# RWKV-7 scan and a quick-GELU MLP on one core: padded rows for the channel sums of the decays, and another order for the first third of a hand-listed program

## The chip, the cores and the metric

The kernel runs on one core of one Trainium2 chip. The metric is the time of one execution on the device in microseconds; lower is better. TensorE (PE in the profile) multiplies and writes to PSUM; VectorE (DVE), ScalarE (ACT) and GpSimd (POOL) do the elementwise work; SyncE (SP) issues nearly all DMA transfers from one queue.

## The reference

For each of 4 batches and 8 heads a 40x40 state runs over 768 steps; its readings, put side by side, go through an MLP with the activation h * sigmoid(1.702 h).

```python
B, H, S, D = 4, 8, 768, 40
for t in range(S):
    y[:, :, t] = einsum('bhd,bhde->bhe', r_t, state)
    Sa = einsum('bhde,bhe->bhd', state, a_t)
    state = state * w_t[:, :, None, :] - einsum('bhd,bhe->bhde', Sa, b_t) + einsum('bhd,bhe->bhde', v_t, k_t)
x = y.transpose(0, 2, 1, 3).reshape(3072, 320)
h = x @ w_in                                  # 320 x 2048
out = (h / (1 + exp(-1.702 * h))) @ w_out     # 2048 x 320
```

All is float32 but the two weights, which arrive in float64.

## The kernel before

**Units.** The steps are cut into 12 chunks of 64, the batches into 2 pairs; a chunk of a pair is a unit, 24 in all, unit i being chunk i // 2 and pair i % 2. For each unit the kernel loads the decays w, and a, k, b, r, v, and takes the logarithm of w (line 536). `by_time` and `by_channel` (lines 552 and 560) add up the logarithms along the chunk by matmuls with the triangular mask `edges`, once with time on the partitions (psum tile ps_cum) and once with channels (ps_cumc). Exponentials of the sums give FT, GT, wch and G, with which a, b, k are scaled (lines 629 to 637). `by_channel` is used for the units below BY_PE = 4; the others load w a second time in channel order (wc) and use a scan on VectorE. Then come the scores A, RV and N (ps_A, ps_RV, ps_N), five levels of a blockwise inverse (ps_level), its off-diagonal parts (ps_Q, ps_T), the solve (ps_B, ps_X) and the reading (ps_y), whose result x goes to DRAM and comes back transposed as xT_all. In units 0 to 3 a level is a matmul group from PT and EX into ps_level, a transpose of ps_level on DVE into EX (line 733) and a copy to PT on ACT or DVE (line 794). Unit i needs the state that unit i - 2 left (ps_zT, ps_rz). When both units of a chunk are back, the MLP of the chunk runs: ps_up, the activation, ps_down.

**Weights.** The float64 weights come as eight pieces of 1.3 MB, each by four transfers into a raw buffer, and are made into float32 by one ACT instruction (line 457, "rebased"), three on DVE (461, 465, 469) and one on POOL (473, "joined"). The raw buffers are shared: pieces 0, 5 and 7 use one, 3 and 6 another.

**The order.** Every step is a task with a number, given by the order in which the program adds it. The text ORDER lists all 2,709 tasks in the order in which they are issued; a token is the task's number, the letter of its engine (p TensorE, a ScalarE, d VectorE, g GpSimd, s SyncE) and, for a task that uses PSUM, which of four pairs of banks it gets. Each engine runs its tasks strictly in this order. For SyncE the digit behind the letter is a window: with 4, this transfer waits until all but the last four issued ahead of it have landed; without a digit it waits for none.

The numbers that matter here:

| tasks | what they are |
| --- | --- |
| 0, 1, 2, 91 | load of w for units 0 to 3 |
| 5, 6, 7, 8, 9 and 10 to 14 | loads of ak, b, rv, v (RV), time (k and b by time) for units 0 and 1 |
| 15 to 18, 24 to 27, 33 to 36, 42 to 45 | loads of weight pieces 0 to 3, four quarters each |
| 19, 28, 37, 46, 55, 64, 73, 82 | "rebased" of weight pieces 0 to 7 |
| 23, 32, 41, 50, 59, 68, 77, 86 | "joined" of weight pieces 0 to 7 |
| 87, 88 and 141, 142 | ps_cum and ps_cumc of units 0 and 1 |
| 93, 94, 95, 96, 97 and 148 to 152 | scaling of a, b, k (by channel) and k, b (by time), units 0 and 1 |
| 100 and 101 | ps_RV of unit 0 and its masking on DVE |
| 103 and 158 | ps_N of units 0 and 1 |
| 107, 110, 113, 116, 119 / 162 ... 174 / 290 ... 302 | levels of units 0, 1 and 2 |
| 126, 128, 134, 136 / 181, 183, 189, 191 | ps_Q, ps_T, ps_X, ps_y of units 0 and 1 |
| 138, 139, 140 / 193, 194, 195 | x, x to DRAM, x read back, units 0 and 1 |
| 351, 353, 363 | ps_A, ps_RV and the second level of unit 3 |
| 196 to 205, 207 to 216 | first two quarters of ps_up of the first chunk |

Of the kernel before, what the change touches and what calls it, by code (L numbers as in the profile page):

```python
# [121 lines left out]
200p2 58d 468p1 201p2 368d0 469a 473s 202p2 476s 203p2 67d 387p0 477s 470a1 490d 204p2 68g 480s 339a 205p2 369p1 388d0 206a2  # L122
215p3 371d1 218p0 219p0 56d 472s4 216p3 483g 71s4 220p0 217a3 471d 81s4 221p0 482d 79s 311p2 222p0 370a1 223p0 224p0 312d2 225p0
340d 372p3 229p1 478s4 376a3 230p1 57d 378a3 324p2 560s4 377a3 59g 226p0 78s4 375a3 325d2 231p1 73a 232p1 227p0 373d3 326p2 374d
228a0 389p3 484g 479s3 327d2 338s4 240p0 529d 390a3 481g 328d2 379p3 233p1 380a3 329d 234p1 391p2 485g 241p0 556s4 392d2 80s4
# [118 lines left out]
2690p3 2691p3 2692p3 2693p3 2694p3 2698p1 2695a3 2699p1 2696d3 2700p1 2697s 2701p1 2702p1 2703p1 2704p1 2705p1 2706d1 2707d1  # L244
2708s
"""


@with_exitstack
def rwkv7_gelu_quick(ctx: ExitStack, tc: tile.TileContext, time_d, v_d, w_d, wc_d, ak_d, b_d, rv_d, w_in, w_out, out):  # L250
    nc = tc.nc
    H, D, S = 8, 40, out.shape[0] // 4
    DM = H * D
    C = 64
    MID = C // 2
    NU = time_d.shape[0]
# [8 lines left out]
    BY_PE = 4  # L265
# [110 lines left out]
    for t in logw_t:  # L376
        nc.gpsimd.memset(t[:, DM:], 0.0)
# [772 lines left out]
```

## Time and profile before

| | us |
| --- | --- |
| median of 3 runs | 680.82 (679.36 to 682.35) |
| the profiled execution's own time | 679.49 |
| its span, first to last instruction | 677.7 |
| TensorE matmul busy | 649.6 (96%) |
| VectorE, ScalarE, GpSimd busy | 449.7, 329.1, 175.7 |
| DMA | 69.74 MB, mean 103 GB/s |

Matmul busy time is the union of pipelined instructions, so a full TensorE is not TensorE at its peak. Nearly every matmul of the program is recorded on line 301, a helper, and every DMA on line 331, so groups are told apart by their tiles. The profile counts two instructions for each float32 matmul of the program. "Idle before" in a row is the time for which the engine had nothing to run ahead of this group, and what ended it.

### The profile page before, as it was taken

Reading aid. Unit: us, or ns where it says so; the run is one execution under the profiler, and the core shown is the slowest. Engines: PE = TensorE matmul, PEld = TensorE weight load, DVE = VectorE, ACT = ScalarE, POOL = GpSimd, SP = SyncE. Lnnn points to the kernel's source line nnn. Section 1 sums busy time; section 2 is a strip of 40 time slices with the busy share of each in tenths; the row PEclk is TensorE's granted clock in tenths of the full one; section 3 lists DMA queues with packets and bytes.
Section 4 is the critical chain, followed back from the end, with each engine's and each line's share of the span. In section 5 each row is a group of like instructions: output and inputs, shape, how many; then the busy total and the mean of one; then the engine's idle time right before and its main releaser. Section 6 shows DMA issues by size and latency. Waiting matters only on the chain.

```text
span 677.7 us, 42447 instructions
## 1 busy us (share of the span) xinstructions
PE 649.6 (96%) x19616; PEld 568.7 (84%) x19616; DVE 449.7 (66%) x916; ACT 329.1 (49%) x681; POOL 175.7 (26%) x201
## 2 busy tenths in 40 slices
PE   5777999999999999999999999999999999999997
PEld 4667787787999997888888899999889798799896
DVE  5777779777867668757776687868656766675001
ACT  3676745634564655654545445455344454263010
POOL 6541443324123123123113211322411421300000
PEclk9979999999999999999999999999999999999999
DMA  6875753415324314432404513513412411200200
GB/s 208 295 255 160 226 172 97 129 42 152 107 64 131 94 58 124 114 107 65 124 14 131 149 35 108 155 33 107 140 38 62 130 53 45 69 15 14 60 13 21
DMA packets 35473, 69.74 MB, mean 103 GB/s; under 512 B 5472, under 2 KB 14816, under 8 KB 35296
## 3 DMA queue, kind: packets, MB, share of 16 engines
q1 hardware_dynamic: 35216, 66.99, 32.9%
q8 instruction: 154, 2.52, 1.6%
q14 instruction: 23, 0.19, 0.1%
q10 hardware_dynamic: 80, 0.04, 0.0%
HBM read 59.15 MB, written 7.86 MB: 99 GB/s over the span
## 4 chain that ended last, share of the span: by engine, by line
PE 88%; DMA 6%; DVE 2%; issue 1%; SPq 1%; ACT 1%; DVEq 0%; ACTq 0%
PE ps_up L301 31%; PE ps_down L301 29%; PE ps_level L301 8%; PE ps_y L301 5%; PE ps_B L301 4%; PE ps_X L301 2%; PE ps_N L301 2%; PE ps_rz L301 1%; PE ps_RV L301 1%; PE ps_A L301 1%; PE ps_zT L301 1%; SPq L331 1%; DMA w_sb<-in_w_in 1%; PE ps_cum L301 1%; PE ps_T L301 1%
## 5 line engine op out<-in xcount | busy, mean ns | idle before, releaser
L301 PE MATMUL ps_up<-xT_all,w_sb 64*64 64x256 f32 x3840 | 253.3, 377 | 2.1 <-issue 1.3
L301 PE MATMUL ps_down<-w_sb,g 64*64 64x320 f32 (+1 forms) x3200 | 241.5, 419 | 0.2 <-ACT zr L879 0.2
L301 PEld LDWEIGHTS ps_up<-xT_all,w_sb 64*64 64x64 f32 x3840 | 170.8, 133 | 18.8 <-issue 2.1
L301 PEld LDWEIGHTS ps_down<-w_sb,g 64*64 64x64 f32 x3200 | 142.5, 133 | 31.6 <-issue 0.4
L1000 ACT ACTIVATE g<-ps_up 128x1024 f32<-128x1024 f32 x48 | 49.2, 1025 | 46.3 <-PE ps_up L301 45.8
L719 POOL TENSOR_TENSOR EX<-ES,quads 128x512 f32<-128x512 f32 x30 | 39.7, 1324 | 116.4 <-DVE ES L712 77.7
L761 ACT COPY W<-ps_level 128x512 f32<-128x512 f32 x56 | 32.8, 585 | 67.7 <-PE ps_level L301 66.0
L301 PEld LDWEIGHTS ps_level<-W,EX 64*64 64x64 f32 x2560 | 60.0, 134 | 5.4 <-DVE T L840 0.2
L763 DVE TENSOR_TENSOR E<-two,ps_level 128x256 f32<-128x256 f32 x80 | 33.1, 415 | 36.5 <-ACT W L761 32.3
L301 PE MATMUL ps_level<-W,EX 64*64 64x64 f32 (+1 forms) x2560 | 56.8, 217 | 0.0
L717 ACT ACTIVATE EX<-ES,quads 128x256 f32<-128x256 f32 x82 | 37.2, 501 | 31.9 <-DVE ES L712 31.3
L629 POOL TENSOR_TENSOR ak<-ak,FT 128x512 f32<-128x512 f32 x17 | 23.0, 1353 | 77.2 <-DMA ak<-in_ak 54.4
L301 PEld LDWEIGHTS ps_level<-PT,EX 64*64 64x64 f32 x1280 | 30.7, 138 | 11.5 <-DVE EX L733 3.3
L301 PE MATMUL ps_level<-PT,EX 64*64 64x64 f32 (+2 forms) x1280 | 32.5, 234 | 6.9 <-DVE EX L733 5.0
L712 DVE STREAM_TRANSPOSE ES<-E 128x256 f32<-128x256 f32 x80 | 35.3, 443 | 4.4
L301 PE MATMUL ps_y<-RV,kh 64*64 64x104 f32 (+1 forms) x768 | 35.4, 247 | 0.9 <-DVE M L917 0.9
L301 PE MATMUL ps_y<-M,bh 64*64 64x104 f32 (+1 forms) x768 | 35.5, 247 | 0.7 <-DVE M L917 0.5
L901 ACT COPY B<-ps_B 128x416 f32<-128x416 f32 (+1 forms) x35 | 17.2, 493 | 34.4 <-PE ps_B L301 34.2
L301 PEld LDWEIGHTS ps_y<-RV,kh 64*64 64x64 f32 x768 | 29.6, 133 | 3.2 <-DVE M L917 1.5
L917 DVE TENSOR_TENSOR M<-ps_X,later 128x832 f32<-128x832 f32 (+1 forms) x24 | 23.9, 995 | 10.2 <-PE ps_X L301 10.0
L301 PE MATMUL ps_B<-RV,A 64*64 64x104 f32 (+1 forms) x768 | 29.2, 252 | 0.8 <-issue 0.8
L637 POOL TENSOR_TENSOR kh<-time,G 128x320 f32<-128x320 f32 x18 | 16.2, 901 | 51.2 <-PE ps_y L301 34.6
(133 smaller groups left out, 1099.0 us busy)
## 6 DMA issues: line engine op xcount, KB each, us to landing
ak<-in_ak SPq DMA_DIRECT2D x48, 160.0 KB
rv<-in_rv SPq DMA_DIRECT2D x48, 160.0 KB
time<-in_time SPq DMA_DIRECT2D x24, 320.0 KB
xT_all<-x_dram SPq DMA_DIRECT2D x48, 160.0 KB
wc<-in_wc SPq DMA_DIRECT2D x20, 264.0 KB
logw<-in_w SPq DMA_DIRECT2D x24, 160.0 KB
RV<-in_v SPq DMA_DIRECT2D x24, 160.0 KB
b<-in_b SPq DMA_DIRECT2D x48, 80.0 KB
```

The lines of the kernel that those rows point to most:

```text
L301: nc.tensor.matmul(o, lhsT, rhs, start=start, stop=True, skip_group_check=True)
L331: begun.append(queue.dma_start(dst, src).ins)
L629: plan.add(R, {"DVE": 690.0, "POOL": 1270.0, "sbuf": True}, lambda t: of(t.engine).tensor_mul(ahT(), ahT(), FT_of(i)), reads=T("ak", "FT") ...
L637: plan.add(R + 4, {"POOL": 870.0, "DVE": 490.0, "sbuf": True}, lambda t, n=n, dst=dst: of(t.engine).tensor_mul(dst(i)[:, :, :D], by_head(t ...
L712: plan.add(rank, dve(256), lambda t: nc.vector.transpose(ES(n), source(t)), writes=[key("ES", n, 6)], **reads)
L717: nc.scalar.activation(dst[:, :, h], ES(n), ACT.Copy, scale=quads[:, h, :1])
L719: of(t.engine).tensor_mul(dst, ES(n).unsqueeze(2).to_broadcast([128, 8, 2, 32]), quads.unsqueeze(1).to_broadcast([128, 8, 2, 32]))
L761: plan.add(rank, any2(512), lambda t: copy(t.engine)(tiles_of(W(n + 1)), blocks(psum(t, ""), 64)), writes=[key("W", n + 1, 5)], pair=pair)
L763: plan.add(rank, dve(256), lambda t: nc.vector.tensor_sub(tiles_of(E(n + 1)), every(two32, [128, 2, 4, 32]), blocks(psum(t, ""), 64)[:, :, ...
L901: plan.add(R, any2(4 * wide), lambda t: copy(t.engine)(dst(), some(psum(t, "")[:, :, :208])), writes=[("Bv", i)] if x and c > 0 else T("B" ...
L917: plan.add(R + 1, dve(8 * wide), lambda t: nc.vector.tensor_tensor(M_of(i)[:, :, :wide].rearrange("p (j b) n -> p b j n", b=2), some(psum( ...
L1000: plan.add(-45, {"ACT": 1030.0, "table": "gelu"}, lambda t: nc.scalar.activation(g_of(c * NQ + q).rearrange("p m r n -> p r m n"), psum(t, ...
```

## The change

The w of units 0 to 3 comes from a new input, `in_apart`, in which each head's 40 channels are padded to 64 with ones, and lands in the tile that the later units use for wc. The logarithm is taken of the 40 channels of each head. Two neighbouring heads now stand in 128 columns, so `by_channel` issues 8 matmuls of 64 rows by 128 columns for 16 of 64 by 64. The three tiles for w lose their tail of 24 columns and its zeroing. The first 800 places of ORDER hold the same tasks in another sequence, with 71 of them on another engine and with other windows on SyncE; from the 801st on the sequence is the same, and from the 1,038th the bank pairs too.

The diff, with ORDER cut to its first lines (12 of 47 before, 17 of 47 after):

```diff
--- before.py
+++ after.py
@@ ORDER @@
-0s 8s 1s4 5s 102a 7s 6s 3a 9s 157a 87p0 88p1 10s 89a1 100p2 90a0 95d 13s4 4a 11s 93d 12s 101d2 98p3 2s 94d 97d 17s 103p1 16s 96d
-142p0 15s 104a1 105d1 141p2 143a0 106d 99d3 107p1 144a2 18s4 148g 132p3 108a1 109d1 155p0 45s4 149d 27s 150g 156d0 158p2 14s4
-110p1 159a2 160d2 91s4 130p0 161d 19a 24s4 112d1 162p2 111a1 22d 26s4 25s 163a2 113p1 20d 131a0 152g 164d2 34s4 92a 272s 21d
-165p0 114a1 151g 271s 147a 153p2 115d1 273s 166a0 167d0 116p1 23g 28a 154d2 262p0 343s 117d1 263p2 133a3 342s 264a2 118d1 168p3
-36s 31d 33s 119p1 276g 169a3 170d3 35s 120d1 42s 122a1 171p2 277d 278g 121a 43s 124d1 123a1 126p3 173d2 125a1 127d3 285a 29d
-128p1 172a2 44s4 286p3 30d 54s4 37a 174p2 129d1 32g 51s4 288d3 134p1 178a2 146s4 175d2 145s 265a0 135d1 176a 187p0 289d 136p1
-275s4 179a2 266g 61s 38d 138d1 188a0 341s 139s 287a3 181p0 39d 185p3 40d 137a1 177a2 290p1 313d 180a2 182a0 53s4 280g 279g 274s
-186a3 183p2 292d1 281p0 291a1 333p3 41g 184d2 332p1 282d0 189p2 334a3 60s4 345s 314p0 190d2 316a0 346d 355a 191p3 347d 315d0
-193d3 356p2 344s2 62s 140s 194s 195s4 192d3 293p0 335a1 358d2 46a 283p3 359d 317p1 294a0 295d0 349g 318a1 284d3 360p0 269a 348d
-350g 296p1 336d 361a0 362d0 319p3 383d 357a2 297a1 298d1 384p0 321p2 49d 320a3 299p1 385a0 47d 322a2 63s4 363p3 300a1 301d1
-323d2 386a0 302p1 364a3 365d3 353p0 351p2 306a1 48d 267s3 207p3 52s3 307a1 305d1 208p3 50g 268s3 64a 303d1 209p3 352d2 210p3
-211p3 354d0 308a1 196p2 304a 212p3 65d 197p2 213p3 72s3 214p3 70s3 270d 55a 309p1 337s3 198p2 69s4 366p0 310a1 66d 199p2 367a0
...
+102a 0s8 5s3 3a 88p3 87p2 89a3 6s6 94d 8s 1s8 90a2 93d 95d 103p1 9s 96d 4a 142p0 104a1 7s8 97d 141p3 16s 100p2 105d1 106d 107p1
+11s4 101d2 143a0 149d 144a3 98p3 157a 10s 148d 158p0 14s6 109d1 150g 99d3 160d0 151g 108a1 161d 110p3 15s 17s 18s 12s8 152g
+112d3 13s 19a 22d 130p1 131a1 162p2 164d2 25s8 155p1 111a3 159a0 156d1 163a2 113p3 114a3 20d 21d 165p2 132p0 153p1 24s6 166a2
+27s8 115d3 167d2 116p3 26s 2s 28a 275s8 168p2 45s4 154d1 118d3 92a 262p1 36s6 271s6 133a0 263p0 170d2 33s 117a3 119p3 23g 61s
+31d 169d2 264a0 265a1 120d3 29d 121a 171p0 266g 122d3 126p2 125d3 272s6 268s 172a0 124d3 278g 127d2 123a3 43s 173d0 128p2 174p3
+180a3 52s8 177a3 129d2 134p0 187p2 277d 285a 276g 286p1 178a3 188a2 287a1 135d0 136p0 30d 175d3 176a 181p2 51s8 137a0 32g 288d1
+280g 179d3 35s 185p3 186a3 289d 182d2 183p1 138d0 184d1 290p2 91s8 147a 189p3 292d2 279g 34s6 332p1 343s6 345s 37a 291a2 355a
+333p2 334a2 190d3 342s 335a1 281p0 282d0 313d 273s 347d 274s 191p3 192d3 314p0 316a0 315a0 341s 346g 293p1 139s8 193d3 295d1 44s
+336d 383d 356p3 358d3 54s 359d 317p2 294a1 296p0 348g 267s 357d3 318a2 298d0 42s6 60s3 46a 47d 297a0 194s6 38d 360p2 361a2 283p1
+140s8 384p3 339a 299p0 300a0 284d1 39d 362d2 146s8 349g 195s6 319p1 320a1 301d0 62s 386a3 321p1 340d 322d1 385a3 53s 323d1 350g
+145s 302p0 307a0 305a0 344s 196p3 197p3 40d 49d 306a0 198p3 303d0 41g 353p2 55a 308a0 476s 199p3 200p3 201p3 354d2 304a 363p1
+365d1 480s4 351p2 63s4 478s 352d2 207p0 208p0 269a 209p0 48d 364a1 210p0 211p0 270d 202p3 309p1 468p2 212p0 64a 310a1 65d 213p0
+50g 366p1 368d1 214p0 560s6 215p0 216p0 67d 203p3 469a 204p3 481d 470a2 205p3 66d 70s 367a1 218p1 219p1 220p1 58d 217a0 206a3
+369p2 221p1 222p1 311p3 223p1 71s2 371d2 473s 387p0 224p1 370a2 312d3 324p3 372p2 388a0 377a2 483g 378a2 375a2 229p0 230p0 376a2
+225p1 226p1 227p1 228a1 68g 81s 325d3 326p3 373d2 374a 490a 56d 57d 391p2 72s8 328d3 471d 389p1 327d3 231p0 232p0 392a2 486p3
+233p0 393d2 59g 69s3 477s 234p0 379p2 73a 390a1 329d 79s6 487d3 235p0 236p0 482d 237p0 558s 78s4 238p0 380a2 381p1 338s8 240p2
+241p2 239a0 80s6 82a 529d 530p3 74d 484d 488p0 75d 242p2 337s 531a3 382d1 479s6 76d 83d 84d 532a3 330s6 394p1 491p3 494a3 243p2
...
 @with_exitstack
-def rwkv7_gelu_quick(ctx: ExitStack, tc: tile.TileContext, time_d, v_d, w_d, wc_d, ak_d, b_d, rv_d, w_in, w_out, out):
+def rwkv7_gelu_quick(ctx: ExitStack, tc: tile.TileContext, time_d, v_d, w_d, apart_d, wc_d, ak_d, b_d, rv_d, w_in, w_out, out):
     nc = tc.nc
     H, D, S = 8, 40, out.shape[0] // 4
     DM = H * D
@@ -372,9 +372,7 @@
         select(edges[q], ALU.is_gt, 0, 1, -1.0)
         select(edges[p.start + MID:p.stop], ALU.is_gt, -MID, 1, 0.0)
     incl = edges[:, 1:]
-    logw_t = several("logw", [128, DM + 24])
-    for t in logw_t:
-        nc.gpsimd.memset(t[:, DM:], 0.0)
+    logw_t = several("logw", [128, DM])
 
     quads, within = single("quads", [128, 2, 32]), single("within", [128, 2, 32])
     nc.gpsimd.memset(quads, 0.0)
@@ -493,12 +491,13 @@
     ak_of, b_of, rv_of = lambda i: ak_t[i % 2], lambda i: b_t[i % 2], lambda i: rv_t[i % 2]
 
     RV_of = lambda i: buf("RV", i, [128, 13, 8, 8])
-    logw_of = lambda i: logw_t[i % 3][:, :DM]
+    logw_of = lambda i: logw_t[i % 3] if i >= BY_PE else apart(i).rearrange("p (h d) -> p h d", h=H)[:, :, :D]
 
     wc_of = lambda i: buf("wc", i, [128, 2, 8 * 33])
+    apart = lambda i: wc_of(i).rearrange("p n h -> p (n h)")[:, :H * 64]
 
     def load_w(i):
-        for name, of, src, n in (("wc", wc_of, wc_d, 528), ("logw", logw_of, w_d, DM))[i < BY_PE:]:
+        for name, of, src, n in (("wc", wc_of, wc_d, 528), ("logw", logw_of, w_d, DM)) if i >= BY_PE else (("wc", apart, apart_d, H * 64),):
             plan.add(-2 if i == 2 else 10 * i - 30, {"SP": 350.0}, lambda t, of=of, src=src: transfer(t, of(i), src[i]),
                      writes=[(name, i)], size=128 * n * 4)
 
@@ -535,7 +534,7 @@
                 nc.scalar.activation(wc_of(i), wc_of(i), ACT.Ln)
             nc.scalar.activation(logw_of(i), logw_of(i), ACT.Ln)
         plan.add(10 * i - 30, {"ACT": 1000.0 if i >= BY_PE else 470.0, "table": "exp"}, go,
-                 reads=[("logw", i)] + ([("wc", i)] if i >= BY_PE else []) + ([("exps", i - 2)] if i > 1 else []), writes=[("log", i)])
+                 reads=[("wc", i)] + ([("logw", i)] if i >= BY_PE else []) + ([("exps", i - 2)] if i > 1 else []), writes=[("log", i)])
 
         def sums(t):
 
@@ -550,20 +549,20 @@
         R = 10 * i - 9
 
         def by_time(t):
-            ps, lw = psum(t, "ps_cum"), logw_of(i)
+            ps, lw = psum(t, "ps_cum"), logw_of(i) if i < BY_PE else logw_of(i).rearrange("p (h d) -> p h d", h=H)
             for n in (1, 0):
                 for b in BITS:
                     u = b ^ n
-                    mm(ps[HALF[u], b, :160], incl[HALF[b]], lw[HALF[b], n * 160:(n + 1) * 160], True)
-        plan.add(R, pe((1, 160)), by_time, reads=T("log"), uses=T("logw"), room=T("G"), writes=T("cum"), pair=("cum", i))
+                    mm(ps[HALF[u], b, :160].rearrange("p (h d) -> p h d", d=D), incl[HALF[b]], lw[HALF[b], 4 * n:4 * n + 4], True)
+        plan.add(R, pe((1, 160)), by_time, reads=T("log"), uses=T("logw") if i >= BY_PE else T("wc"), room=T("G"), writes=T("cum"), pair=("cum", i))
 
         def by_channel(t):
 
             ps = psum(t, "ps_cumc")
             for u, f in product(BITS, BITS):
-                for b, e in QUARTERS:
-                    o, h = (2 * u + f) * 65, head(e, f, b, u) * D
-                    mm(ps[HALF[e], b, o:o + 65], logw_t[i % 3][HALF[b], h:h + 64], edges[HALF[b]], o == 0)
+                for b in BITS:
+                    o, h = (2 * u + f) * 65, head(0, f, b, u)
+                    mm(ps[:, b, o:o + 65], apart(i)[HALF[b], 64 * h:64 * h + 128], edges[HALF[b]], o == 0)
 
         def exp_of_product(t):
             tables(t)
@@ -579,7 +578,7 @@
                     nc.scalar.activation(ends[:, n, b], sums[:, b, :, 64 * n].rearrange("p (u f) -> p u f", u=2), ACT.Exp, scale=2.0 * n - 1.0)
 
         if i < BY_PE:
-            plan.add(R, pe((4, 65)), by_channel, reads=T("log"), uses=T("logw"), room=T("FT", "GT"), pair=("cumc", i))
+            plan.add(R, pe_wide((4, 65)), by_channel, reads=T("log"), uses=T("wc"), room=T("FT", "GT"), pair=("cumc", i))
 
         def exp_channel(t):
             tables(t)
@@ -1127,10 +1126,14 @@
     w_in = pieces(w_in.reshape(8, 128, 640))
     w_out = pieces(np.asarray(moe_w_out).reshape(16, 128, 320))
 
+    by_time = time_tile(w, False)
+    apart = np.ones((4, 128, H, 64), np.float32)
+    apart[..., :D] = by_time[:4].reshape(4, 128, H, D)
     arrays = {
         "in_time": np.ascontiguousarray(np.stack([time_tile(k, True), time_tile(b, True)], 2)),
         "in_v": beside(v),
-        "in_w": time_tile(w, False),
+        "in_w": by_time,
+        "in_apart": apart.reshape(4, 128, H * 64),
         "in_wc": halves(channel_tile(w, "e", "ubf")),
         "in_ak": np.ascontiguousarray(np.stack([channel_tile(a, "e", "ubf"), channel_tile(k, "e", "ubf")], 2)),
         "in_b": channel_tile(b, "e", "ubf"),
```

More of the change, by code (lines that the diff above doesn't have):

```diff
@@ L122 @@
[L122 to L125, printed above, removed]
@@ new lines @@
+395d1 493d3 492d3 496d 556s8 396p1 489d0 397d1 398d1 559s3 251p3 252p3 331s6 77g 244p2 495g 85d 485d 497a 498p1 500d1 548p0 570d
+474a 86g 245p2 557s4 549a 550a0 399d 499a1 253p3 562d 246p2 568p1 569d1 472s 533p0 564g 561g 247p2 501d 534a0 248d2 249d2 553s4
+400s3 254p3 255p3 571p0 574a0 475d 572d0 535p2 256p3 565g 573d0 694p1 552s 563g 401s2 536d2 551g 576d 695a 696a1 257p3 258p3
+250s3 259d3 537p2 566p0 577g 554a 706s 700a 260d3 567d0 575g 578p1 580d1 609d 402p3 403p3 581d 582d 538a2 404p3 405p3 406p3
@@ new lines @@
+781s 786d 833d 735d3 547s6 784s8 736d 460p0 461p0 737d 793p1 782s8 462p0 788g 734d3 794d1 787d 738p2 739d2 777s 758p1 463p0
+456s8 464p0 759a1 712p3 740d2 741d 778s 790g 465a0 789d 918p1 919a 466d0 795p2 797d2 921g 626s8 627s3 650p0 713d3 798d2 796d2
+800d 932d 930s8 742a 651p0 652p0 653p0 1006s8 834p3 836a3 835d3 654p0 655p0 656p0 657p0 467s6 801g 658p0 779a 799d 920a1 924a
+925d 923s6 760p3 761a3 659p0 660a0 762p2 763a2 802p3 804d3 805d 628p1 629p1 806g 630p1 631p1 803d3 632p1 743p3 749d3 746d3 633p1
@@ new lines @@
+664p3 998a 1002s 978d 938p1 946g 665p3 939d1 666p3 772s 667p3 668p3 829p1 669p3 999a0 1000d 1001s 830d1 670p3 1003a 1011d 676p2
+671a3 1004d 831p1 841p0 677p2 832d1 1005s 842d0 936p1 843d0 678p2 937d1 844p0 679p2 845d0 947p1 1010g 680d2 846p0 948a1 681d2
+1012d 682s 683p2 847d0 1013g 1008s 848d0 1019p3 1014g 949d1 684p2 1022a3 1230s 849d 1233s 979p0 685p2 980a0 950d 850s 1020d3
+981a0 951g 1142p1 1021d3 686p2 1024d 1143a 1147s 1023d 1025g 982p0 1057d 687p2 1152s 952p3 851s 983a0 1145g 688p2 1156d 1146s
@@ L157 @@
+1042a2 972d3 877p0 973d3 878p0 879p0 1043d2 1017p1 1044d 974p3 1045a 880p0 1018d1 1231s 881p0 975a3 1164p2 882p0 1167a2 1165d2
+1375s 976p1 883p0 1166d2 896p3 1169d 1168g 884a0 977d1 885p2 1170a 1046p0 989p1 1049a0 886p2 1050a0 990d1 887p2 1051a0 888p2
 1052a0 889p2 1047d0 991p1 1048a 1065p0 992d1 1158g 1153s 890p2 1159d 1066a0 891p2 892p2 1067d0 1378s 893p2 1202d 1063p0 993d1
```

47 lines of the change are left out of this document (16 added, 31 removed).

## The prediction, made before the changed kernel ran

> **What bounds the kernel now.** I read the page first, the slices of the span in particular.
>
> ```profile
> PE   5777999999999999999999999999999999999997
> ...
> PEclk9979999999999999999999999999999999999999
> DMA  6875753415324314432404513513412411200200
> ```
>
> One slice is 17 us. TensorE is full from the fifth slice on and not in the first four, and only there do the DMA engines come near full. Then I looked up where the reordered tasks run. Both lists hold the same tasks in the same sequence from the 801st on; its next TensorE task, 646, ended at 193.46 us in this execution. The first matmul of the MLP ran at 66.48 us. So I cut the span at these two times (PE, PEld, DVE, ACT, POOL busy, then the granted clock, DMA share and GB/s):
>
> ```profile
> 0.00:15.00 15.00, 6.75 (x180) 5.77 (x184) 8.31 (x16) 6.12 (x22) 8.32 (x41) 1.00 0.64 191
> 15.00:45.00 30.00, 22.22 (x776) 19.45 (x776) 21.98 (x37) 19.14 (x47) 13.66 (x9) 0.89 0.89 298
> 45.00:66.48 21.48, 16.54 (x752) 14.90 (x753) 16.48 (x30) 14.86 (x38) 6.52 (x5) 1.00 0.55 155
> 66.48:193.46 126.98, 124.99 (x3685) 102.67 (x3676) 97.48 (x188) 68.92 (x136) 43.90 (x36) 1.00 0.42 128
> 193.46:677.70 484.24, 479.12 (x14249) 425.95 (x14240) 305.45 (x648) 220.03 (x444) 103.34 (x111) 1.00 0.27 79
> ```
>
> Of 66.48 us of head TensorE is busy 45.51 and idle 20.97. From 66.48 to 193.46 it idles 1.99 us, and the 484 us behind that run unchanged in both kernels. What the change can win is in the head; it can lose anywhere before 193.46. What ends the waits of the head is seen in the waits of VectorE and in the timelines of TensorE and of SyncE's queue:
>
> ```profile
> DVE EX L733 <- ACT PT L794: 7.7, 6, 2.4
> ...
> DVE RV L660 <- PE ps_RV L301: 1.9, 1, 1.9
> ```
>
> ```profile
> 14.91 1.56 PE L301 MATMUL ps_level<-PT,EX 64*64 64x96 f32 x32 [0.67 <-DVE EX L733]
> ...
> 66.48 2.48 PE L301 MATMUL ps_up<-xT_all,w_sb 64*64 64x256 f32 x40
> ```
>
> ```profile
> 56.67 0.84 SPq L331 DMA_DIRECT2D x_dram<-x  x2
> 61.39 1.09 SPq L331 DMA_DIRECT2D xT_all<-x_dram  x2
> ```
>
> The head is a chain, not a full engine: score N of units 0 and 1, five levels each (TensorE, then a transpose on DVE and a copy on ACT, one behind the other since both read the same PSUM pair), the solve, x to DRAM and back, and then the MLP can start.
>
> **Part 1, the sums two heads at a time.** 32 matmul instructions a unit become 16, in four units. The 32 of one unit took 1.12, 1.12, 0.69 and 0.65 us. No row of before shows 64 rows by 128 columns. Lower end: time goes with the count, 0.33 us less for each unit. Upper end: a weight of twice the columns takes twice as long and two such tiles instead of four run side by side, 0.65 us more each. So -1.3 to +2.6 us of TensorE over four units, and only unit 0's lies on the head's chain with nothing beside it. I take 0, between the ends, as the number of streamed columns for each tile position stays the same.
>
> [...]
>
> The other edits of this part: the first transfer is 256 KB for 160, at 298 GB/s 0.3 us more; against it the sums no longer wait for the zeroing of the tails (logarithm done at 3.65, sums from 3.80) and the channel sums go first instead of 0.56 us behind the time sums (3.80 and 4.36). I keep the first exponential at its 5.56. The logarithm still covers 320 elements a row (0.46 us). Unit 4's and 5's w no longer wait for the slots of units 1 and 2; nobody waited for these.
>
> **Part 2, the new order: the start of unit 0.** Before, task 94 (b of unit 0, 0.68 us) stands on DVE behind task 101 (RV), which waits until 10.16 us for r and v to land and be multiplied; score N could start at 11.71 and the first level at 14.91. Now ak and b are the second and third loads and 94, 93 stand first on DVE. From the exponential's end at 7.04 less its last part, GT is there at about 6.7: 94 and 93 to 8.1, N 1.1 to 9.2, beside it 95, 96, 97 (0.69 + 0.48 + 0.48) to 9.8, then PV 0.69 and EX 0.71: first level at 11.2, 3.7 earlier.
>
> **Unit 1.** Its a and b products now run on DVE (0.72 for 1.28 on POOL) ahead of unit 0's next transpose. N of unit 1 stands before unit 0's second level on TensorE, so that level waits for ak of unit 1, which is at 2.65 MB in SyncE's queue: at the 191 GB/s of the first 15 us, 13.9. Then 0.7 + 0.7 + 0.8: second level at 16.2 (19.83 before).
>
> **Weights on the ACT queue.** This is what the new list pays with. The rebase of a weight (1.4 us on ACT, tasks 19, 28, 37, 46) now stands 2 to 5 places behind the issue of its last quarter (19, 23, 23 and 78 before), so ACT will stand still until it lands, with the copies PT of the levels queued behind. Counting the queue by sizes and going by 191 GB/s for 15 us (2.87 MB) and 298 after: weight 0 (3.97 MB) at 18.7, weight 1 (5.77) at 24.7, weight 2 (10.13) at 39.4, weight 3 (13.18) at 49.6. Behind weight 0 stand the copies of B 0.5 and PT 0.8: third level of unit 0 at 21.5 (23.55). Behind weight 1 stand 0.5 + 0.5 + 0.8: its last level at 28.0 (30.83). So it keeps 2.8 of the 3.7 us.
>
> **To the end of unit 1.** Before, unit 1's end shared DVE and ACT with unit 2's levels, and the granted clock was 0.50 for a stretch:
>
> ```profile
> 35.00:40.00 5.00, 4.28 (x118) 4.12 (x120) 3.54 (x7) 3.79 (x8) 2.86 (x1) 0.50 0.93 308
> ```
>
> Some 4.6 us of solid matmuls ran in it, at double price: 2.3 us. From the last level of unit 0 I add rows: ES 0.45 (behind a copy of 0.94 and 0.8 of weight 1 on DVE), spread 0.9: Q at 30.9 (34.51); QT, T21, T and unit 1's last level: X at 34 (38.63); M 1.0, y; unit 1's Q at 38.3, its X at 41 (48.36), y from 43.1 to 45.1 (51.90), x at 46.5 (53.30). That is 6.8 earlier; 2.3 of it is the clock, and if the clock falls again it comes back and the gain is 3.7 instead of 6. In the 5 us ahead of the fall PE was busy for 3.03 of 5.00. [...]
>
> **To the first MLP matmul.** Three strands. Transfers: x of unit 1 is at 13.68 MB in the queue: 51.3 landed; from the issue of the read-back to the first use it was 5.1 us (61.39 to 66.48): 56.4. Levels of unit 2, which now come behind y of unit 1: weight 3 at 49.6 + 1.4 holds PT 0.8, then a level 1.1, 0.7 + 0.8 and the last level 0.9: 56.3. DVE: the tasks listed ahead of the first MLP matmul add up to 47.6 us by their own rows (47.1 before); from 6.7 that is 54.3 if it never idles, or 51.9 without the 2.4 of tasks 340, 322 and 323 (1.3 + 0.5 + 0.6), which the last level doesn't need. It will idle, as the walk above shows at several places; with 6 us of it the three strands end together, and I take 57.5.
>
> **Sum.** 66.48 - 57.5 = 9.0 us. Three TensorE tasks of unit 3 (363, 353, 351) that stood ahead of the first MLP matmul now come behind it: 0.90 + 0.47 + 0.47 = 1.8 back. Behind it, DVE and POOL still have weights 2 and 3 to finish, which before were done but for 3 us, and weight 7, loaded into the buffer that weight 5 leaves, has 45 list places from there to its rebase for 100 before: I give back 1.2. Gain 6 us: 679.49 - 6 = 673.5 for this execution, which lies 1.3 under the median of the three runs, 680.82; on the median 674.8. Half a per cent, 3.4 us, is about what a measurement of this kernel can tell from no change.
>
> **Rivals.** *The head stays as long.* DVE idled 19.7 of 66.48 us; my sum needs that cut to about 10. If each wait only changes its name and idling falls by 5, the first MLP matmul is at 62, the gain 66.5 - 62 - 1.8 - 1.2 = 1.5: 679.3. For it: every level still needs DVE, then ACT. Against: the first wait (RV before b) is gone by the list.
> *ACT stands behind the weights (slower).* The place is task 46 in front of unit 2's third copy. The price hangs on the rate: if the 191 GB/s of the first 15 us held on, 13.18 MB land at 69.0, the first MLP matmul is 6.7 later at 75.7, and the kernel loses 9.2 + 1.8 + 1.2 = 12.2 us: 693.0. At before's mean over the head, 228 GB/s, it would be 57.8 + 6.7 = 64.5, a loss of 1.0; under 219 GB/s (60.2 + 6.7 = 66.9) the loss passes 3.4. Against: 298 GB/s at a share of 0.89 in the stretch that had most under way, and now up to eight transfers are under way where four were.
> *The strands meet better*: transfers at 298 throughout, no clock fall: first MLP matmul at 54, gain 9.5: 671.3.
>
> **Chances.** Forecast 0.55, better 0.17, head as long 0.12, ACT behind the weights 0.16, of which some 0.02 end within half a per cent; of the forecast 0.02 do too. So faster 0.70, same 0.16, slower 0.14. The likeliest case alone spans 672 to 677. The range takes in the better case and the head as long, and some of the slower one: 670 to 685.
>
> **What the profile after would show.** First level at about 11 us, b before RV on DVE; ps_cumc in 64 matmuls for 128; first ps_up at 55 to 60; PE busy near 45 us up to there and idle about 12; a DMA share of 0.85 or more from 15 us to 45; ACT waiting for DMAs ahead of w_sb. Wrong if the first ps_up is past 63, or if the stretch from it to task 646 takes over 131 us (127 before plus the 1.8 and 1.2).

## The result, and the profile after

The kernel after takes 690.05 us (median of 6 runs, 688.24 to 691.03) for 681.59 of the kernel before on the same chips (6 runs, 679.36 to 687.13): the ratio is 1.0109 (95% interval 1.0065 to 1.0152). It is slower, where 674.8 was forecast. The profiled execution took 691.03 us, the longest of the six; its span is 688.9. One execution of a later experiment (hybrid), the profiled one, took 1126.07 us at a granted clock of 0.563 and is left out of that kernel's ratio.

The page of after, the same slices as before:

```profile
PE   6778899899999999999999999999999999999997
...
PEclk9888999999999999999999999999999999999999
DMA  7976462305323513432404413413421421200200
```

TensorE is full only from the sixth slice on (the fifth before), and its clock is below 0.9 in three of the first four slices. The stretches, cut as before at the first ps_up (67.63 us) and at the end of task 646 (203.22); columns as in the prediction:

```profile
0.00:15.00 15.00, 8.53 (x148) 7.66 (x152) 8.39 (x16) 6.91 (x24) 6.79 (x37) 1.00 0.68 198
15.00:45.00 30.00, 22.48 (x716) 20.67 (x712) 19.83 (x35) 15.04 (x35) 9.25 (x8) 0.77 0.89 282
45.00:67.63 22.63, 18.66 (x697) 17.14 (x693) 18.68 (x37) 14.40 (x30) 9.24 (x7) 0.85 0.63 198
67.63:203.22 135.59, 129.29 (x3784) 103.55 (x3780) 103.86 (x187) 67.82 (x140) 47.17 (x36) 0.99 0.38 117
203.22:688.90 485.68, 481.15 (x14248) 425.40 (x14240) 305.70 (x649) 220.24 (x443) 103.98 (x111) 1.00 0.27 79
```

The head is 1.2 us longer, not 9 shorter; the stretch behind it is 8.6 longer (135.6 for 127.0); the common rest is 1.4 longer. The clock column (1.00 in the first row, here and in the prediction) needs care: the first clock record is at 17.91 us in before and at 15.94 in after, and the column counts the time ahead of it as full. There a matmul of ps_N takes 311 ns, as it does in the stretches recorded at 0.50, for 218 at 1.00. So TensorE ran at half clock up to the first record, in both kernels. TensorE's timeline shows where an early lead went:

```profile
4.08 1.97 PE L301 MATMUL ps_cumc<-edges,wc 64*128 64x65 f32 x16 [4.08 <-ACT wc L535]
...
13.69 1.50 PE L301 MATMUL ps_level<-PT,EX 64*64 64x96 f32 x32
...
22.37 0.38 PE L301 MATMUL ps_level<-PT,EX 64*64 64x96 f32 x2
24.12 1.39 PE L301 MATMUL ps_level<-PT,EX 64*64 64x96 f32 x27 [1.38 <-issue]
```

Unit 0's first level starts 1.2 us earlier than before (14.91), its third, at 22.37, 1.2 (23.55). Then that third level stops after two matmuls, for nothing that the profile shows. The waits of TensorE up to the first ps_up, the longest of them, have such "issue" rows second:

```profile
PE ps_cumc L301 <- ACT wc L535: 4.1, 1, 4.1
PE ps_level L301 <- issue: 3.7, 2, 2.3
```

**What these waits are.** The page of after lists the DMA queues:

```profile
q1 hardware_dynamic: 35216, 67.38, 32.5%
q8 instruction: 154, 2.52, 1.6%
```

q8 moves 154 packets of 16 KB, and the trace of before has 39,519 records of TensorE (weight loads, matmuls and its sequencer), 256.6 for each packet. Counted from 0 in order of start, in all 13 traces read here, every record ahead of which TensorE stood for over 0.9 us, and which holds no semaphore, has a number of 193 plus a multiple of 256; before has 154 records with such a number, as many as packets. From this I take the packets to be blocks of TensorE's own instructions, and these records to be the crossings from one block into the next, the packet behind a crossing being the block for the next one. From one record to the next TensorE stood for over 0.9 us at 52 crossings, and every time it went on between 1.24 and 1.61 us after the packet of its block had ended. The pause at 22.74 to 24.12 is one: the crossing ahead of it was at 17.77, the packet ran from 21.77 to 22.86.

From 15 us to 45, at a DMA share of 0.89 in both, a packet started on average 1.63 us after its crossing in before, 2.75 in after. Idle time at crossings up to task 646 is 3.3 us in before, 7.0 in after. One "issue" wait is of another kind: 1.83 us in front of a ps_up at 126.74, in after and (1.43) in after_w4 alone, ends when VectorE has emptied a ps_down, for which it had waited 4.12 us for the store of ob.

### The profile page after: what moved, and what is told of

It is laid out like the page before. It is cut to its first block, busy times and chain, and to the rows that moved or that the text cites. A ratio compares the mean times of both kernels' runs of the same rounds, so it can differ in the third digit from the quotient of the medians.

```text
span 688.9 us, 42287 instructions
## 1 busy us (share of the span) xinstructions
PE 660.1 (96%) x19552; PEld 574.4 (83%) x19552; DVE 456.5 (66%) x918; ACT 324.4 (47%) x672; POOL 176.4 (26%) x198
## 4 chain that ended last, share of the span: by engine, by line
PE 89%; DVE 4%; issue 2%; DMA 2%; ACT 1%; SPq 0%; POOL 0%; POOLq 0%; ACTq 0%; DVEq 0%
PE ps_up L301 29%; PE ps_down L301 29%; PE ps_level L301 10%; PE ps_y L301 4%; PE ps_B L301 4%; PE ps_X L301 2%; PE ps_A L301 2%; PE ps_rz L301 2%; PE ps_RV L301 2%; PE ps_N L301 1%; PE ps_zT L301 1%; PE ps_Q L301 1%; PE ps_T L301 1%; DMA rv<-in_rv 1%; PE ps_cum L301 1%
## 5 line engine op out<-in xcount | busy, mean ns | idle before, releaser
L301 PEld LDWEIGHTS ps_up<-xT_all,w_sb 64*64 64x64 f32 x3840 | 170.6, 134 | 22.8 <-issue 4.1
L718 POOL TENSOR_TENSOR EX<-ES,quads 128x512 f32<-128x512 f32 x32 | 42.3, 1324 | 123.7 <-DVE ES L711 89.1
L760 ACT COPY W<-ps_level 128x512 f32<-128x512 f32 x55 | 32.2, 586 | 79.7 <-PE ps_level L301 66.8
L301 PE MATMUL ps_level<-W,EX 64*64 64x64 f32 (+1 forms) x2560 | 58.2, 218 | 0.4 <-issue 0.4
L716 ACT ACTIVATE EX<-ES,quads 128x256 f32<-128x256 f32 x74 | 33.7, 503 | 28.7 <-DVE ES L711 28.2
L301 PE MATMUL ps_level<-PT,EX 64*64 64x64 f32 (+2 forms) x1280 | 35.8, 246 | 4.3 <-issue 3.7
L301 PEld LDWEIGHTS ps_level<-PT,EX 64*64 64x64 f32 x1280 | 34.0, 149 | 7.0 <-issue 4.1
L628 POOL TENSOR_TENSOR ak<-ak,FT 128x512 f32<-128x512 f32 x15 | 20.1, 1343 | 65.7 <-DMA ak<-in_ak 36.6
L900 ACT COPY B<-ps_B 128x416 f32<-128x416 f32 (+1 forms) x34 | 16.7, 490 | 28.9 <-PE ps_B L301 28.6
L301 PE MATMUL ps_B<-RV,A 64*64 64x104 f32 (+1 forms) x768 | 28.9, 252 | 1.2 <-ACT B L900 0.7
L301 PEld LDWEIGHTS ps_B<-RV,A 64*64 64x64 f32 x768 | 26.1, 137 | 4.3 <-ACT B L900 0.9
```

Of the source, the lines that this page charges most:

```text
L301: nc.tensor.matmul(o, lhsT, rhs, start=start, stop=True, skip_group_check=True)
L628: plan.add(R, {"DVE": 690.0, "POOL": 1270.0, "sbuf": True}, lambda t: of(t.engine).tensor_mul(ahT(), ahT(), FT_of(i)), reads=T("ak", "FT") ...
L716: nc.scalar.activation(dst[:, :, h], ES(n), ACT.Copy, scale=quads[:, h, :1])
L718: of(t.engine).tensor_mul(dst, ES(n).unsqueeze(2).to_broadcast([128, 8, 2, 32]), quads.unsqueeze(1).to_broadcast([128, 8, 2, 32]))
L760: plan.add(rank, any2(512), lambda t: copy(t.engine)(tiles_of(W(n + 1)), blocks(psum(t, ""), 64)), writes=[key("W", n + 1, 5)], pair=pair)
L900: plan.add(R, any2(4 * wide), lambda t: copy(t.engine)(dst(), some(psum(t, "")[:, :, :208])), writes=[("Bv", i)] if x and c > 0 else T("B" ...
```

## The experiments

Four theories stood against each other: (1) code blocks that come late, because of deep SyncE windows or of where the boundaries fall; (2) the wide matmuls; (3) the sequence itself with its in-order waits; (4) the clock. All ratios are to the kernel before on the same chip. The other columns come from one profiled execution each: the start of task 646; TensorE's busy time, its idle time at code-block crossings and its other idle time up to there; the granted clock up to the first ps_up, as recorded; the time at half clock up to 646, with the stretch up to the first clock record (13.0 to 24.0 us) counted in. Executions of one kernel differ among each other by some 2 us (standard deviation over 171 of them), so a single profile says where time goes, and the ratio how much.

| kernel | ratio (95% interval) | 646 at | busy | idle at crossings | other idle | head clock | half clock |
| --- | --- | --- | --- | --- | --- | --- | --- |
| before | 1 | 192.70 | 170.1 | 3.3 | 19.4 | 0.95 | 24.7 |
| after | 1.0109 (1.0065 to 1.0152) | 202.07 | 178.0 | 7.0 | 17.1 | 0.85 | 39.8 |
| order_only | 1.0087 (1.0060 to 1.0115) | 198.76 | 173.9 | 9.3 | 15.5 | 0.82 | 37.6 |
| order_w4 | 1.0053 (1.0023 to 1.0084) | 195.16 | 172.3 | 5.5 | 17.4 | 0.95 | 27.0 |
| after_w4 | 1.0100 (1.0076 to 1.0124) | 198.89 | 176.6 | 3.4 | 18.9 | 0.92 | 26.0 |
| after_narrow | 1.0072 (1.0049 to 1.0096) | 197.46 | 170.8 | 9.9 | 16.8 | 0.87 | 30.1 |
| sums_only | 1.0085 (1.0053 to 1.0117) | 196.40 | 173.3 | 7.4 | 15.8 | 0.93 | 28.1 |
| sums_level | 1.0048 (1.0021 to 1.0075) | 196.86 | 175.7 | 5.8 | 15.4 | 0.93 | 27.8 |
| narrow_old | 1.0017 (0.9992 to 1.0042) | 196.62 | 175.3 | 3.8 | 17.5 | 0.88 | 44.5 |
| before_shift16 | 1.0073 (1.0045 to 1.0101) | 199.50 | 175.8 | 9.0 | 14.8 | 0.91 | 36.7 |
| before_shift32 | 1.0062 (1.0031 to 1.0094) | 194.90 | 171.4 | 8.7 | 14.9 | 0.98 | 21.7 |
| before_w8 | 1.0033 (1.0006 to 1.0059) | 194.95 | 168.7 | 8.4 | 17.9 | 0.98 | 21.6 |
| before_w3 | 1.0026 (1.0003 to 1.0050) | 197.82 | 173.4 | 3.7 | 20.8 | 0.95 | 30.6 |
| hybrid | 1.0055 (1.0033 to 1.0076) | not read | | | | | |

Two things of this table hold for all that follows. In the six kernels with the old sequence and sums of 64 by 64, busy (less the 1.03 and 1.88 us of the tiny matmuls that two of them add) goes with the time at half clock: 0.30 us for each us (correlation 0.95). And idle at crossings is not a price by itself: over the 13 kernels the other idle is shorter where it is longer (correlation -0.73). In before the two add up to 22.7 us, in after to 24.1.

**order_only**: the kernel before with the new list.

```diff
--- before
+++ order_only
-ORDER = """ ... old """
+ORDER = """ ... new """
```

> The kernel before with the new ORDER alone: units 0 to 3 load w unpadded and make the channel sums by 16 matmuls of 64x64, and everything else of the list is the new one. The order costs by itself (its deeper SyncE windows, and code blocks for TensorE that arrive late behind them): slower than before by 5 to 7 us, first ps_up near 66, idle of TensorE at the code-block boundaries as long as in the kernel after. The wide sums cost: of the 8.5 us that the kernel after lost, 2 to 2.6 are missing here, with the sums of a unit back at 1.1 us or less; by this theory alone order_only would be within 2 us of before. The clock: nothing follows from the edit, and the time goes with the granted clock of the run.

5.9 us slower (0.0087 of 681.7): the list costs by itself. First ps_up 67.18. The other idle time is 3.9 shorter than in before, which is what the list was good for; idle at crossings is 6.1 longer. Its own walk up to there fits the prediction well: first level 11.25 (11.2 forecast), second 16.30 (16.2).

**sums_only**: the kernel after with the old list.

```diff
--- after
+++ sums_only
-ORDER = """ ... new """
+ORDER = """ ... old """
```

> The kernel after with the old ORDER: padded rows and wide sums, list of before. If the wide sums cost what their rows show (1.97, 1.97, 1.11 and 1.11 us for 1.12, 1.12, 0.69 and 0.65): slower than before by 0.9 (only unit 0's lie on the chain) to 2.6 us (all four). If the cost of the change is all in the order: the same as before within 1 us, first ps_up at 66 to 67.

5.8 us slower, more than either theory gave. The instructions of ps_cumc, first before and then after (count, shortest, median and longest duration of one in ns, first and last start, form):

```profile
L301 PE MATMUL ps_cumc<-edges,logw x96: 218/312/312, 4.4 to 29.4; 64*64 64x65 f32 x96
```

```profile
L301 PEld LDWEIGHTS ps_cumc<-edges,wc x32: 283/330/335, 4.0 to 11.8; 64*128 64x128 f32 x32
L301 PE MATMUL ps_cumc<-edges,wc x32: 414/414/473, 4.1 to 11.9; 64*128 64x65 f32 x32
```

One wide matmul lasts 414 ns for 312, and the group of unit 0 or 1 takes 1.97 us for 1.12. Both units run ahead of the first clock record, so at half clock. At full clock (recorded 1.00), in unit 2, a wide matmul lasts 272 ns for 218, and the group, before and then after:

```profile
28.91 0.69 PE L301 MATMUL ps_cumc<-edges,logw 64*64 64x65 f32 x32
```

```profile
31.48 1.11 PE L301 MATMUL ps_cumc<-edges,wc 64*128 64x65 f32 x16
```

In TensorE's busy time to task 646, instruction by instruction, ps_cumc has 5.95 us here, 5.95 in after_w4 and 6.02 in after, for 2.90 in before: 3.1 more for half the instructions. That leaves 2.7 of the 5.8.

**after_w4** and **after_narrow**: the kernel after with shallow windows, and with sums of 64 by 64 from the padded rows.

```diff
--- after
+++ after_w4
-102a 0s8 5s3 ... 6s6 ... 1s8
+102a 0s4 5s3 ... 6s4 ... 1s4
--- after
+++ after_narrow
-                for b in BITS:
-                    o, h = (2 * u + f) * 65, head(0, f, b, u)
-                    mm(ps[:, b, o:o + 65], apart(i)[HALF[b], 64 * h:64 * h + 128], edges[HALF[b]], o == 0)
+                for b, e in QUARTERS:
+                    o, h = (2 * u + f) * 65, head(e, f, b, u)
+                    mm(ps[HALF[e], b, o:o + 65], apart(i)[HALF[b], 64 * h:64 * h + 64], edges[HALF[b]], o == 0)
```

> The kernel after with each SyncE window of 5 to 9 in ORDER cut to 4, so that at most four transfers are under way as in the list of before. Code blocks late behind deep windows: the waits that the profile calls issue fall from some 7 us back to 3 up to task 646, and the kernel is 3 to 5 us faster than after. The order itself or the wide sums: within 1.5 us of after. If the bytes of the head need the deep windows: slower than after by 2 us or more, with more waits for DMAs in the head.

Half of it came. Idle at crossings did fall from 7.0 to 3.4, and task 646 started 3.2 us earlier in the profile; the ratio is lower by only 0.0009, far inside its interval. Other idle rose by 1.8. Some transfers came later: ScalarE's waits for the transfers of weights in the first 72 us add up to 6.8 us, for 2.2 in after.

> The kernel after with the channel sums as 16 matmuls of 64x64 (two instructions each in the profile) from the same padded rows, in place of 8 of 64x128. Wide sums cost: sums of a unit back at 1.1 us or less, first level of unit 0 some 0.8 earlier, kernel 1 to 2.6 us faster than after. Everything in the order: within 0.5 us of after. It also shifts where the code-block boundaries of TensorE fall by 64 instructions in all, so a change of either sign at single waits of that kind is expected.

2.5 us faster than after (1.0072 for 1.0109), not resolved by the intervals; busy time is 7.2 shorter in the profile, 2.7 of it in ps_cumc. With the same instructions as order_only it comes out alike. By this pair theory 2 is about a third of the loss; two other pairs, below, give more.

**before_shift32** and **before_shift16**: the kernel before, with 32 or 16 tiny matmuls while TensorE has nothing to do.

```diff
--- before
+++ before_shift32
+    def shift(ps, n):
+        for k in range(n):
+            r, h = QUARTERS[k % 4]
+            mm(ps[HALF[h], r, :1], early[HALF[r]], early[HALF[r], :1], True)
...
+    early = single("early", [128, 64])
+    nc.vector.memset(early, 1.0)
     padded(nc.vector, ak_t[0])
...
             ps, lw = psum(t, "ps_cum"), logw_of(i)
+            if i == 0:
+                shift(ps, 32)
```

> The kernel before with 32 tiny matmuls more (64 rows, one column, from a small tile of ones, into PSUM that the first sums overwrite) while TensorE still waits for the first w; a memset of that tile (64 columns) stands first on VectorE. Nothing else differs, but every later code-block boundary of TensorE falls 128 instructions earlier in the program. Code blocks: the waits that the profile calls issue, 3.3 us up to task 646 in before, land on other matmuls and differ in sum, by 1 to 4 us in either direction, and the time follows them; TensorE's other waits in the head keep their places. If code blocks cost nothing: within 0.5 us of before at task 646.

> As before_shift32, with 16 tiny matmuls for 32: the boundaries fall 64 instructions earlier than in before. Code blocks: another sum of stalls at boundaries, between 3 and 9 us up to task 646, and the time follows it (0 to 5 us slower than before). If the 4 us of before_shift32 came from something that its tiny matmuls or the memset did: half of it here, about 2 us.

4.2 and 5.0 us slower. The tiny matmuls ended at 2.93 and delayed the first sum by 0.07 (3.87), and half as many cost no less, so their own time isn't it. Waits of TensorE up to 70 us, shift by 32:

```profile
PE ps_level L301 <- issue: 4.6, 2, 2.9
...
PE ps_B L301 <- issue: 1.4, 1, 1.4
```

and in before, up to its first ps_up, the rows of this kind:

```profile
PE ps_B L301 <- issue: 0.8, 1, 0.8
PE ps_N L301 <- issue: 0.7, 1, 0.7
...
PE ps_level L301 <- issue: 0.3, 1, 0.3
```

Idle at crossings goes from 3.3 to 8.7 and 9.0. Moving the boundaries this way goes with a loss of 0.6 to 0.7%, over half of the whole change's; before has them in good places. A shift by a whole block of 256, which would keep the boundaries and add the same kind of matmuls, was not run. In the shift by 16 the profiled execution also had 12.0 us more at half clock than before.

**before_w8** and **before_w3**: the windows alone.

```diff
--- before
+++ before_w8
-0s 8s 1s4 ... 13s4 ... 18s4
+0s 8s 1s8 ... 13s8 ... 18s8
--- before
+++ before_w3
-0s 8s 1s4 ... 13s4 ... 18s4
+0s 8s 1s3 ... 13s3 ... 18s3
```

> The kernel before with every SyncE window of 4 raised to 8, nothing else. Code blocks late behind deep windows: in the head the packet of a block starts some 2 to 4 us after the boundary was crossed for 0.9 to 2 in before, stalls at boundaries rise from 3.3 us by 2 to 4 up to task 646, and the kernel is 2 to 4 us slower. If deep windows only bring bytes earlier: no slower than before, with the waits for DMAs (RV 3.0, N 1.0) the same or shorter.

> The kernel before with every SyncE window of 4 cut to 3. Code blocks: shorter from the crossing of a boundary to the block's landing, stalls at boundaries below the 3.3 us of before, and up to 2 us faster. If bytes bind instead: weights and x land later, waits for DMAs rise, and the kernel is 1 to 4 us slower.

2.2 and 1.8 us slower. With windows of 8 the packets start 2.56 us after the crossing (15 to 45 us; 1.63 before), idle at crossings is 8.4, and the wait rows of the head show it:

```profile
PE ps_level L301 <- issue: 4.1, 3, 2.5
...
PE ps_B L301 <- issue: 1.4, 2, 1.2
```

With windows of 3 the packets are no earlier (1.68), and the other idle rises by 1.4; ScalarE's waits for transfers of weights in the first 72 us go from 0.4 us to 4.0. So 4 lies between two small losses. The depth of the windows alone does not set how late a packet starts: order_only and order_w4 have the same 2.06 and 2.05, and the shift by 16, with windows of 4, has 2.87. These are means of a few packets each.

**narrow_old** (old list, padded rows, sums of 64 by 64) and **sums_level** (sums_only, with 8 tiny matmuls ahead of each wide group, so that TensorE's instructions are as many as before).

```diff
--- sums_only
+++ sums_level
             ps = psum(t, "ps_cumc")
+            for r, h in QUARTERS * 2:
+                mm(ps[HALF[h], r, :1], early[HALF[r]], early[HALF[r], :1], True)
```

> The old ORDER with w of units 0 to 3 from padded rows, and the channel sums as 16 matmuls of 64x64 as in before: the layout without the wide matmuls and without the new list. TensorE's instructions and their code blocks are those of before. The wide matmuls were what cost in sums_only (they alone took 6 us there): within 1 us of before, first exponential at 5.2 for 5.56. If the layout costs (256 KB for 160 in the first transfer, the logarithm on a strided view): slower than before by over 1.5 us.

> sums_only (padded rows, wide sums, old ORDER) with 8 tiny matmuls of one column ahead of each of the four wide groups, so that TensorE issues as many instructions as in before and its code-block boundaries fall where they fall in before. The tiny ones cost some 0.06 us each (1.88 us for 32 in before_shift32), 0.5 for each group. If the 6 us that sums_only lost were the wide matmuls alone (3.1 us by their own rows in TensorE's busy time): as slow as sums_only or 1 to 2 us slower. If half of it was the shifted boundaries: 1 to 3 us faster than sums_only, with stalls at boundaries back at 3 to 4 us up to task 646.

The layout costs nothing that can be told from no change (1.0017). Instead of the 5.2 expected, the first exponential came at 5.84: with the old list the sums by time go first. With the boundaries back in place sums_level is 2.5 us faster than sums_only, though it runs 32 matmuls more; the intervals overlap, and its profile has 1.6 us less at crossings but task 646 no earlier (196.86 for 196.40). By the ratios about 3 us of what sums_only lost would be the wide matmuls, and the rest would go with shifted boundaries; this is not resolved.

**order_w4**: order_only with windows of at most 4.

```diff
--- order_only
+++ order_w4
-102a 0s8 5s3 ... 6s6 ... 1s8
+102a 0s4 5s3 ... 6s4 ... 1s4
```

> The kernel before with the new ORDER and every SyncE window of 5 to 9 in it cut to 4 (old layout, old sums): the new sequence without deep windows and without wide sums. Code blocks: stalls at boundaries fall from 9.3 us in order_only to 3 to 5 up to task 646, and the kernel is 3 to 5 us faster than order_only, 1 to 3 slower than before. If the sequence itself is what costs (work put behind the first MLP matmul, in-order waits on ScalarE and VectorE): as slow as order_only, 5 to 6 over before, at short stalls. If the bytes need the deep windows: slower than order_only.

2.3 us faster than order_only by the ratios, which again overlap; in the profiles idle at crossings falls from 9.3 to 5.5, and task 646 comes 3.6 earlier. Here the list shows what it can do, in the stretches up to the first ps_up and from there to task 646:

```profile
0.00:63.90 63.90, 45.80 (x1601) 40.19 (x1605) 45.66 (x85) 36.12 (x89) 25.98 (x54) 0.95 0.75 233
63.90:195.16 131.26, 126.30 (x3768) 103.47 (x3764) 102.31 (x185) 67.32 (x140) 47.77 (x36) 1.00 0.41 126
```

The first ps_up is at 63.90, 2.6 us earlier than before. What follows takes 131.3 us to the start of task 646, for 126.2 in before: 2.1 more of busy time, for the work that comes later now, and 2.9 more idle. The waits of that stretch:

```profile
PE ps_A L301 <- DMA rv<-in_rv: 1.7, 1, 1.7
PE ps_y L301 <- DVE M L917: 1.2, 1, 1.2
PE ps_A L301 <- issue: 1.1, 1, 1.1
```

**hybrid**: the first 180 places of the new list with shallow windows, then the old sequence.

> Old layout and old sums; the first 180 places of the new ORDER (to the end of unit 1's reading, windows at most 4), then what is left in the old sequence, with PSUM bank pairs given anew where they collide. The order that gets units 0 and 1 done early is good for 1 to 2 us as long as transfers stay few and the old sequence follows: y of unit 1 starts 0.9 us earlier in order_w4 than in before, and the stretch from the first ps_up to task 646 stays at 127 us: 679 to 681, up to 2 us faster than before. If code blocks eat what a denser head wins: same as before within 1 us or slower.

3.7 us slower than before, so the mend doesn't work; its one profile is of the execution of 1126 us, so why stays open. No version here beats the kernel before.

**The clock** (theory 4) is part of it. Over 171 executions, each against its kernel's mean, 0.01 of mean recorded clock goes with 2.5 us (correlation -0.39). The means of after and order_only, 0.9895 and 0.985, lie under those of the same kernels with shallow windows, 0.9937 and 0.9954; before had 0.991 to 0.994 over its runs. By that slope the clock would account for 0.4 to 1.1 us of after's loss, and 1.5 to 2.3 of order_only's; the start ahead of the first clock record is in none of these means. In the profiled execution of after it weighs more: of 7.9 us more busy time 3.1 are ps_cumc, and 15.1 us more at half clock, at the 0.30 above, would be 4.5, most of the rest (ps_level 32.2 for 28.9). Why the half clock lasts longer there is open. Deep windows alone do not bring it: before_w8 has 21.6 us of it for 24.7, and a mean of 0.9928 for 0.9939 in before on the same chip.

**The sum.** By the ratios the sequence itself costs 3.6 us (order_w4). From there to the 7.4 of after two ways lead: deep windows 2.3 and then wide sums 1.5 (by order_only), or wide sums 3.2 and then deep windows 0.6 (by after_w4). What the one costs depends on the other, and each of these steps is about as large as its interval. In the one profile of after, the 9.4 us by which task 646 is later are 3.1 of wide sums, some 4.5 of half clock and 1.4 of idle in all; so how much of the 7.4 is late code blocks, as against the clock, is not settled. Two more comparisons give the wide sums, with the boundaries that they shift, 2.5 (after against after_narrow) and 4.6 (sums_only against narrow_old).

## Why the prediction was wrong, step by step

The step that failed is the walk to the first MLP matmul, 66.48 - 57.5 = 9.0 won: in the profile 1.2 were lost. It had the wide sums at nothing, TensorE's stalls at code blocks at nothing, and 2.3 us of clock as won. The 3.0 given back behind it were 8.6. How the missing 10 us of the head split among these is not settled.

**Part 1, wide sums at 0: the term was mis-sized.** The cost is +0.85, +0.85, +0.42 and +0.46 us by the rows of the four units, 2.6 in all, where 0 was taken because the streamed columns stayed the same. That the recorded upper bound is also 2.6 is chance: both bounds were worked out with 0.65 us for each of the four units, and by their own rows (1.12, 1.12, 0.69, 0.65) half the time and double the time would have been -1.8 and +3.6. The change of shape shows no wait of its own: the 64 by 64 sums behind the wide group start at 5.98, before the group's end at 6.05, which is modelled. The first exponential, which I kept at 5.56, was at 6.09: the sums started at 4.08 and not 3.80, as the larger transfer landed later (the logarithm waited 0.22 us for it and started at 3.51 for 3.19), and took longer (1.97 us for 1.12). In order_only it was at 5.00.

**The start of unit 0 and unit 1: right for the list, spoiled by the sums.** First and second level 11.2 and 16.2 forecast; 11.25 and 16.30 in order_only, 13.69 and 17.75 in after, where unit 1's wide group stands on TensorE ahead of unit 0's first level.

**The later levels: here the walk failed.** Third level 21.5, last 28.0, Q 30.9, X 34 forecast; 22.37, 32.52, 37.47, 41.19 in after. The two long stalls of the head, 1.38 and 2.28 us, lie on this chain, and the walk had none; the rows that tell of them in before (issue, 0.8 and 0.7) had no term in it. The same count of instructions in less time brings the boundaries closer together, and a block took its time: from crossing to crossing, the 52 stalled ones took 3.5 to 6.8 us. Between the two stalls the clock was also at half (22.8 to 29.6 us), where two groups of this level's kind took 1.39 and 1.48 us for 0.89. I had looked at the deep windows only as bytes that come earlier.

**The weights on ScalarE: the rival did not come about.** Before the first ps_up ScalarE stood still for the transfer of a weight once, and TensorE behind it (TensorE's row, then ScalarE's):

```profile
PE ps_RV L301 <- ACT B L900: 1.6, 1, 1.6
```

```profile
ACT w_sb L455 <- DMA extra<-in_w_in: 2.2, 1, 2.2
```

The copy of B stood behind the rebase of weight 0 (19.86, forecast 18.7). Weights 2 and 3, forecast at 39.4 and 49.6, were rebased from 47.71 and 59.69, without a wait for their transfers: their turn in ScalarE's list came late. The rate held, 282 GB/s from 15 to 45 us; that this rival's 693.0 lies near the measured 690.05 is chance.

**The clock:** the 2.3 us that I had counted as won and flagged came back, and more: 0.85 up to the first ps_up for 0.95, as recorded. The double price was too high, too: a matmul of ps_N takes 311 ns at half clock for 218.

**First ps_up 57.5: 67.63.** Without deep windows and wide sums (order_w4) it came at 63.90, with 4.4 us of idle at crossings up to there. If all of that lay on the chain, it would leave 2 us of the difference to other waits; this was not followed.

**Given back behind, 1.8 + 1.2: the first right, the second too small.** In order_w4 the moved work is 2.1 us and the added idle 2.9; in after 8.6 us are given back, 4.3 of them idle (1.92 at one crossing, the 1.83 in front of a ps_up). Both conditions named as "wrong if" were met: first ps_up past 63, and 135.6 over 131.

## What to carry to other kernels

In these traces TensorE's instructions came in blocks of 256 by DMA, beside the data, and 52 times TensorE got to the end of a block before the next one was there (it got past it 3.5 to 6.8 us after the last crossing). In a stage with dense transfers (here a DMA share of 0.89) and many small matmuls, look for "issue" waits in TensorE's row, and count instructions to see whether they are 256 apart. An edit that changes the number or the place of TensorE's instructions then moves every later boundary (32 tiny matmuls went with 8.7 us of idle at crossings for 3.3); it is best judged against the same boundaries, with tiny matmuls to make up the count. Idle at such crossings is not yet lost time: over the 13 kernels the other idle was shorter where it was longer (correlation -0.73). And look where the clock records begin (here at 13.0 to 24.0 us) before a clock of 1.00 is believed. Last, half the instructions were not half the time here: 16 wide matmuls took 1.11 us for the 0.69 of 32 of 64 by 64.

## What the runs showed of the hardware

- A block of TensorE's code of 16 KB took about 1 us to move (means of 1.07 to 1.13), and execution went on 1.24 to 1.61 us after that (52 stalls in 13 traces). From 75 to 200 us the packet started 0.72 to 1.23 us after the crossing on average, and from 15 to 45 us 1.6 to 2.9 (the DMA share was 0.89 there and 0.37 to 0.39 from 75 to 200, in before and after).
- 16 tiny matmuls ahead of everything, in time that was idle, went with 5.0 us more in a kernel of 680 us (3.1 to 6.9 by the interval).
- TensorE ran at half clock from its first matmul to the first clock record, 13.0 to 24.0 us into the span in 13 traces (ps_N 311 ns, as at a recorded 0.50, for 218 at 1.00); the profile showed 1.00 there.
- A float32 matmul on 64 rows by 128 columns with 65 streamed columns lasted 272 ns for 218 at 64 by 64, and a group of half as many took 1.11 us for 0.69; at half clock 414 for 312, and 1.97 for 1.12.
